# One routing table with 832 slots per expert in place of two tables with 640 and 240

## The chip, the cores and the metric

The kernel runs on one core of one Trainium2 chip. The metric is device time of one execution in microseconds (us), as the median of several runs. Inputs are float32 and float64 arrays (the first mixture's weights are float64 words that the kernel takes apart); the output is float32.

## The reference, cut to what matters

A linear attention with decays gives 3072 tokens of width 384. A first mixture takes the maximum of three products and projects back to 384. A second mixture routes each token to its two best of 8 experts and adds the weighted results:

```python
def _moe2_ref(x, w_gate, w_noise, noise, w1, w2):      # x: 3072 x 384, 8 experts, hidden width 1024
    logits = x @ w_gate
    noisy_logits = logits + np.log1p(np.exp(x @ w_noise)) * noise
    top2 = np.argpartition(-noisy_logits, 2, axis=1)[:, :2]
    # ... top2_w: softmax over the two
    for e in range(E):
        for k in range(2):
            mask = top2[:, k] == e
            h = np.maximum(x[mask] @ w1[e], 0.0)
            out[mask] += top2_w[mask, k, None] * (h @ w2[e])
```

## The kernel before

The program is one long straight line of tiles; a planner orders the instructions of each engine ahead of the run, by the order in the text and by its own durations for each instruction, and sets all semaphores.

First phase. Attention works in 24 half units; 12 units u of 256 tokens go through the first mixture (`ffn`, `proj`, lines 357 to 392). `proj` yields 128 tokens at a time, which an SP DMA writes to a gather table in DRAM (`x2d`), 392 words to a row: the token, then its weight for each expert. Batches b of six such tiles (768 tokens, four batches) are routed by `route_a` to `route_m` (lines 405 to 533), spread over the following units by `side`; the last batch is routed in the written order of the second phase. `route_c` counts, by matmuls, each token's rank among those of its expert; `route_r` adds the counts of the batches before (`base`); `route_h` makes two one-hot forms per tile and choice on DVE (rank within a block of 128, and block with expert, times the token's code); `route_m` multiplies them on TensorE and adds the result into a table `TAB` of [128 slots, block x expert]. `decode` turns the codes into row numbers `IDX` for the gathers and scatters.

Batches 0 to 2 are group 0 with a table of its own, a DRAM table of its own and 640 slots (5 blocks) per expert; batch 3 is group 1, with 240 slots (2 blocks).

Second phase (from line 724). The straight path gives each expert two parts, n = 2e and 2e + 1: part 0 has 384 tokens (blocks 0 to 2 of group 0), part 1 has 496 (blocks 3 and 4 of group 0, then 128 and 112 slots of group 1). For each tile of a part `gather` (line 755, POOL indirect DMA) fetches rows, `turn` (764) transposes them on TensorE and splits them into a high and a low part (ACT, DVE); for each of 8 slices of the hidden width `up` (781) runs 9 matmuls with all the part's tokens as moving columns (3 slices of the width, 3 products of high and low parts); for each tile `down` (800) runs 24 matmuls of 384 columns with the tile's hidden values as stationary operand, scales on ACT and adds the rows to the output by a POOL indirect DMA with accumulation. Each such scatter waits for the one before it. In steady state `up` of part n is interleaved with `down` of part n - 1 and `turn` of part n + 1, and part n + 2 is gathered.

The passage between the phases is written out by hand (lines 817 to 868): five gathers (three of part 0, two of part 1 of expert 0) stand ahead of the last `proj`; batch 3 is routed between the first `up` slices; then come the last two gathers of part 1 and those of part 2.

Slots without a token point at spare rows. An expert with more tokens than its slots is finished by `spill` (line 899) after all else, under a run-time branch on the counts `NBLK`.

Of the kernel before, what the change touches and what calls it, by code (L numbers as in the profile page):

```python
# [28 lines left out]
G_TILES = (18, 6)  # L29
G_HC = (18, 6)  # L30
G_SLOTS = (640, 240)
G_CAP = (5, 2)
G_MID = (1152, 0)   # a code's zero point within the group
G_FIRST = (0, 2304)
# float64's first word at 2 ** -127, as float32
# [4 lines left out]
def gla_moe_kernel(ctx: ExitStack, tc: tile.TileContext, qka, pad, vn, ws, wo, wgn, noise, e1, e2, out):  # L40
# [13 lines left out]
    # ---------------------------------------------------------------- constants  # L54
# [4 lines left out]
    iota = const.tile([128, 144], F32, name="iota")  # L59
    dumpc = const.tile([128, 2, 2], F32, name="dumpc")  # L60
# [4 lines left out]
    TAB = [const.tile([128, NE * G_HC[g]], F32, name=f"tab{g}") for g in range(2)]  # L65
    # rows of the group's gather table, rows of the output; empty slots take one of 128 more rows
    IDX = [const.tile([128, 2, NE * G_CAP[g]], I32, name=f"idx{g}") for g in range(2)]
    NBLK = [const.tile([128, NE], I32, name=f"nblk{g}") for g in range(2)]

    # ---------------------------------------------------------------- attention buffers  # L70
# [21 lines left out]
    # raw weights: two buffers, and three more in w_out's place until that is converted  # L92
# [34 lines left out]
    def late_consts():  # L127
        nc.gpsimd.memset(tri, 1.0)
        nc.gpsimd.affine_select(out=tri, in_=tri, pattern=[[1, 128]], compare_op=OP.is_gt, fill=0.0,
                                base=0, channel_multiplier=-1)  # L130
        nc.gpsimd.memset(ones, 1.0)
        nc.gpsimd.iota(iota, pattern=[[1, 144]], base=0, channel_multiplier=0,
                       allow_small_or_imprecise_dtypes=True)
        # a token's code: its place in its group, so numbered that zero is none's and
        # that float16 holds each
        nc.gpsimd.iota(code[:, 0:9], pattern=[[128, 9]], base=-1152, channel_multiplier=1,
                       allow_small_or_imprecise_dtypes=True)
        nc.gpsimd.iota(code[:, 9:18], pattern=[[128, 9]], base=1, channel_multiplier=1,
                       allow_small_or_imprecise_dtypes=True)
        nc.gpsimd.iota(code[:, 18:24], pattern=[[128, 6]], base=1, channel_multiplier=1,  # L140
                       allow_small_or_imprecise_dtypes=True)
        for g in range(2):
            for s, row in ((0, 128 * G_TILES[g]), (1, NT - G_FIRST[g])):
                nc.gpsimd.iota(dumpc[:, g, s:s + 1], pattern=[[1, 1]], base=row - G_MID[g],
                               channel_multiplier=1, allow_small_or_imprecise_dtypes=True)
            nc.gpsimd.memset(TAB[g], 0.0)

    def zero_rows(q):
# [4 lines left out]
        if q < 2:  # L153
            nc.sync.dma_start(x2d[q][128 * G_TILES[q]:], z)
# [3 lines left out]
    # float64 weights (as words) into a high and a low part of float32r each  # L158
    def dissect(raw, hi, lo):
# [3 lines left out]
        # magnitudes below float32's range become its zero; of those within, the exponent's  # L163
        # three bits after the first say nothing
# [31 lines left out]
    # w_out @ [w_gate | w_noise], as 16 further columns of w_out  # L196
# [51 lines left out]
        # product of a chunk's decays, for each e  # L248
# [71 lines left out]
        # the state before a chunk, decayed to its end  # L320
# [5 lines left out]
    def att_y(j):  # L326
# [13 lines left out]
        else:  # L340
# [6 lines left out]
            # the last pair's rows fill the gaps of the three others  # L347
# [5 lines left out]
    # ---------------------------------------------------------------- first mixture  # L353
# [21 lines left out]
    def proj(u, t):  # L375
# [14 lines left out]
        g = b // 3  # L390
        r = 128 * i - G_FIRST[g]
# [51 lines left out]
    def route_c(b):  # L443
        xf, oh, ob, ex = RT[b]
        g = b // 3
# [8 lines left out]
        # weights of the two  # L454
# [9 lines left out]
        r = 768 * b - G_FIRST[g]  # L464
        nc.sync.dma_start(x2d[g][r:r + 768, DM:XW].rearrange("(j p) e -> p j e", p=128), gs)
        RT[b] = [xf, oh, rk, ct]

    def route_r(b):
        """Rank of a token among those of its expert."""
        xf, oh, rk, ct = RT[b]  # L470
        rb = small([128, 6, NE], "rb")
        if b % 3 == 0:
            nc.vector.tensor_copy(rb, rk)
            nc.vector.tensor_reduce(base, ct.rearrange("p j e -> p e j"), axis=AX.X, op=OP.add)
        else:
# [3 lines left out]
            nc.vector.tensor_add(base, base, cs)  # L479
        rm = small([128, 6, 2, NE], "rm")  # L480
# [14 lines left out]
    def route_h(b, q):  # L495
        """One-hot forms of tiles 2q and 2q + 1: rank within a block, and block with expert."""
        lf, cf, held, ps = RT[b]
        n = NE * G_HC[b // 3]
        for j in (2 * q, 2 * q + 1):
            for k in range(2):  # L500
                A = small([128, 128], "A", F16, 8)
                C = small([128, 144], "C", F16, 8)
# [5 lines left out]
    def route_m(b, q):  # L508
        lf, cf, held, ps = RT[b]
        g = b // 3  # L510
        n = NE * G_HC[g]
# [12 lines left out]
        if g == 1:  # L524
            # left to the general path: none of the slots that the straight one takes
            nc.vector.memset(TAB[1][0:G_SLOTS[1] - 128, NE:2 * NE], 0.0)
        # blocks of the experts that need more than the straight path's slots
        nb = NBLK[g]
# [3 lines left out]
        nc.vector.tensor_scalar(full, base, float(G_SLOTS[g]), None, op0=OP.is_gt)  # L532
        nc.vector.tensor_mul(nb, nb, full)

    def decode(g, t, idx):
# [3 lines left out]
        nc.vector.tensor_scalar(p, t, 0.0, float(G_MID[g]), op0=OP.is_le, op1=OP.add)  # L539
# [319 lines left out]
    up(0, 5)  # L859
    up(0, 6)  # L860
    up(0, 7)
    down(0, 0)
    turn(1, 0)
    down(0, 1)
    turn(1, 1)
# [136 lines left out]
```

## Time and profile before

| what | value |
|---|---|
| runs: median, lowest, highest (3 runs) | 998.48, 997.84, 1000.98 us |
| profiled execution: span from the first to the last instruction | 996.3 us |
| profiled execution's own time beside the span | not listed apart from the span |
| PE (TensorE matmul) busy | 919.3 us (92%) |
| DVE, ACT, POOL busy | 516.7, 392.8, 331.1 us |
| mean granted TensorE clock | 0.985 |
| chain that ended last, by line | `up` L794 23%, `down` L808 22%, `ffn` L365 17% |

Engines: PE is TensorE's matmuls, PEld its weight loads (which overlap PE), DVE VectorE, ACT ScalarE, POOL GpSimd, SP SyncE. A matmul's listed duration holds its pipeline; what it costs in a stream is the distance from one start to the next, which the chain of waits shows for a run of them. A granted clock of 1.00 is TensorE's 2.4 GHz level, 0.50 its 1.2 GHz level. A name such as `psu<-xe,ew` gives the tile written and the tiles read, and L794 is a line of the kernel.

### The profile page before, as it was taken

The numbers are of one execution on the slowest core, as the hardware profiler recorded it, in microseconds if no ns is written. First come the engines' busy times: TensorE is split into PE (matmuls) and PEld (weight loads), VectorE is DVE, ScalarE is ACT, GpSimd is POOL, SyncE is SP. The second block draws the span as 40 slices with busy tenths as digits, with TensorE's granted clock in tenths as the row PEclk, the third lists the DMA queues.
The fourth block names the chain that finished last, engine by engine and source line by source line (L and its number), as shares of the span: only waits on it lengthen the run. The fifth ranks groups of instructions, "written<-read, shape, count | busy, mean of one in ns | idle before, by whom it ended". The sixth has DMA issues, their size and how long they took to land.

```text
span 996.3 us, 17883 instructions
## 1 busy us (share of the span) xinstructions
PE 919.3 (92%) x7186; PEld 870.9 (87%) x7187; DVE 516.7 (52%) x1043; ACT 392.8 (39%) x801; POOL 331.1 (33%) x366
## 2 busy tenths in 40 slices
PE   2367999999999999999899999999999999999994
PEld 2256899999999989999898999999999999999993
DVE  7999847786668865772574233332333332333110
ACT  4544544455445534632534233333333332333220
POOL 5565724322331332213116333323333332321212
PEclk9979999999999999999999999999999999999997
DMA  9642223135224332104434443433444434431122
GB/s 267 180 122 73 57 57 86 44 106 128 70 72 118 83 79 56 33 12 152 155 85 104 118 111 96 111 85 73 111 113 110 99 67 96 106 63 22 23 25 33
DMA packets 37352, 89.64 MB, mean 90 GB/s; under 512 B 8656, under 2 KB 25552, under 8 KB 37264
## 3 DMA queue, kind: packets, MB, share of 16 engines
q1 hardware_dynamic: 25744, 66.59, 23.7%
q0 software_dynamic: 11520, 21.86, 13.0%
q8 instruction: 58, 0.95, 0.4%
q14 instruction: 30, 0.25, 0.1%
HBM read 65.12 MB, written 20.95 MB: 86 GB/s over the span
## 4 chain that ended last, share of the span: by engine, by line
PE 75%; DVE 3%; DMA 3%; issue 1%; ACT 1%; SPq 0%; POOL 0%; POOLq 0%; ACTq 0%; DVEq 0%
PE psu L794 23%; PE psd L808 22%; PE p L365 17%; PE psl L380 5%; PE psx L775 2%; PE psS L292 1%; DMA out_dram<-y,idx 1%; PE psG L308 1%; PE psY L333 1%; DMA xt<-sg 1%; DMA raw<-in_e_dram 1%; PE psT L284 1%; PE psY L334 1%; DVE kh L241 0%; DVE st L318 0%
## 5 line engine op out<-in xcount | busy, mean ns | idle before, releaser
L365 PE MATMUL p<-xt,W 128*128 128x256 f32 x1944 | 254.0, 288 | 10.6 <-DVE m L369 3.9
L794 PE MATMUL psu<-xe,ew 128*128 128x496 f32 (+1 forms) x1152 | 251.8, 367 | 4.5 <-ACT xe L777 4.5
L365 PEld LDWEIGHTS p<-xt,W 128*128 128x128 f32 x1944 | 240.3, 193 | 16.3 <-DVE m L369 4.7
L808 PE MATMUL psd<-ew,he 128*128 128x384 f32 (+1 forms) x1344 | 244.1, 336 | 0.0
L808 PEld LDWEIGHTS psd<-ew,he 128*128 128x128 f32 (+1 forms) x1344 | 234.8, 186 | 1.7
L794 PEld LDWEIGHTS psu<-xe,ew 128*128 128x128 f32 x1152 | 206.7, 189 | 22.9 <-ACT xe L777 5.0
L798 DVE SCALAR_TENSOR_TENSOR he<-psu,he 128x496 fp32r<-128x496 f32 (+1 forms) x128 | 78.4, 614 | 267.9 <-ACT he L797 246.3
L813 POOL DMA_INDIRECT out_dram<-y,idx x56 | 88.4, 1578 | 181.9 <-ACT y L811 166.6
L373 POOL TENSOR_TENSOR H<-m,H 128x256 fp32r<-128x256 f32 x72 | 59.6, 828 | 189.8 <-ACT H L372 183.1
L797 ACT ACTIVATE he<-psu 128x496 fp32r<-128x496 f32 (+1 forms) x128 | 68.9, 539 | 115.7 <-PE psu L794 114.0
L811 ACT ACTIVATE y<-psd,GS 128x384 f32<-128x384 f32 (+1 forms) x56 | 32.5, 581 | 203.3 <-PE psd L808 199.7
L380 PE MATMUL psl<-WO,H 128*128 128x400 f32 x432 | 84.5, 348 | 0.0
L380 PEld LDWEIGHTS psl<-WO,H 128*128 128x128 f32 x432 | 76.8, 188 | 2.0 <-issue 1.3
L742 DVE TENSOR_TENSOR ew<-raw,ew 128x768 fp32r<-128x768 f32 x64 | 57.2, 954 | 33.1 <-ACT ew L741 32.8
L760 POOL DMA_INDIRECT xg<-x2d,idx x56 | 58.0, 1035 | 45.8 <-PE psx L775 21.3
L369 DVE TENSOR_TENSOR m<-p,m 128x256 f32<-128x256 f32 x72 | 30.0, 416 | 61.3 <-ACT m L368 58.1
L779 POOL COPY GS<-xg 128x1 f32<-128x1 f32 (+1 forms) x56 | 11.4, 271 | 135.1 <-DMA xg<-x2d,idx 135.0
L372 ACT CAST H<-m 128x256 fp32r<-128x256 f32 x72 | 29.2, 406 | 66.8 <-DVE m L370 66.8
L368 ACT COPY m<-p 128x256 f32<-128x256 f32 x72 | 26.5, 369 | 68.0 <-PE p L365 59.2
L741 ACT CAST ew<-raw 128x768 fp32r<-128x768 f32 x64 | 48.6, 834 | 3.0 <-DMA raw<-in_e_dram 3.0
L333 PE MATMUL psY<-x,la 128*64 128x64 f32 x384 | 31.0, 234 | 16.3 <-ACT la L323 14.6
L333 PEld LDWEIGHTS psY<-x,la 128*64 128x64 f32 x384 | 26.5, 145 | 20.4 <-ACT la L323 15.5
(152 smaller groups left out, 1081.9 us busy)
## 6 DMA issues: line engine op xcount, KB each, us to landing
raw<-in_e_dram SPq DMA_DIRECT2D x32, 768.0 KB, 6.7
qka<-in_qka_dram SPq DMA_DIRECT2D x48, 289.7 KB, 4.9
out_dram<-z SPq DMA_DIRECT2D x5, 960.0 KB, 5.3
vn<-in_vn_dram SPq DMA_DIRECT2D x24, 192.0 KB, 2.5
x2d<-x2t SPq DMA_DIRECT2D x24, 192.0 KB, 1.9
RAW<-in_ws_dram SPq DMA_DIRECT2D x5, 768.0 KB
wraw<-in_ws_dram SPq DMA_DIRECT2D x4, 768.0 KB, 5.5
xt<-sg SPq DMA_DIRECT2D x72, 32.0 KB, 2.3
```

The source lines that it names most:

```text
L333: nc.tensor.matmul(ps[0:64, p, s], LA[i][:, p, c], X1[j][:, sx], start=True, stop=True)
L365: nc.tensor.matmul(ps, W[:, f, w, a, k], x[:, k, b], start=n == 0, stop=n == 8)
L373: nc.gpsimd.tensor_sub(H[:, u % 2, f, 1], m, hi.bitcast(F32))
L380: nc.tensor.matmul(ps, H[:, u % 2, f, a, 128 * t:128 * t + 128], WOT[0][:, b, f], start=n == 0, stop=n == 17)
L741: nc.scalar.copy(hi, r)
L742: nc.vector.tensor_sub(EW[e, m][:, 1, s], r, hi.bitcast(F32))
L760: nc.gpsimd.indirect_dma_start(out=XG[n, i][0:w], out_offset=None, in_=x2d[g], in_offset=bass.IndirectOffsetOnAxis(ap=IDX[g][0:w, 0, c:c + ...
L794: nc.tensor.matmul(ps, w[:, a, f, k], XE[n][:, k, b], start=i == 0, stop=i == 8)
L797: nc.scalar.activation(hi, ps, AF.Relu)
L798: nc.vector.scalar_tensor_tensor(HE[n][:, f, 1], ps, 0.0, hi.bitcast(F32), op0=OP.max, op1=OP.subtract)
L808: nc.tensor.matmul(ps, HE[n][:, f, a, o:o + m], w[:, b, f], start=j == 0, stop=j == 23)
L813: nc.gpsimd.indirect_dma_start(out=out, out_offset=bass.IndirectOffsetOnAxis(ap=IDX[g][0:m, 1, c:c + 1], axis=0), in_=y, in_offset=None, c ...
```

## The change

The two groups become one: one table `TAB` of 24 blocks per expert, one DRAM table whose first 128 rows are the spare ones, codes around one zero point. The ranks of batch 3 go on where the others end, but not below 384 (`HEAD`), so that the first three blocks hold tokens of batches 0 to 2 only and can be decoded after batch 2. The straight path takes 832 slots per expert: 384 in part 0 and 448 in part 1 (tiles of 128, 128, 128 and 64). The table's width in `route_h` and `route_m` grows with the batch. All four gathers of a part 1 read the later index table; the first two of expert 0 move behind the routing of batch 3. The comments are gone. The core of the diff:

```diff
-G_SLOTS = (640, 240)
-G_CAP = (5, 2)
+NBK = 24
+HEAD = 384
+SLOTS = 832
+CAP = 7
...
-    x2d = [dram.tile([128 * G_TILES[g] + 128, XW], F32, name=f"x2d{g}") for g in range(2)]
+    x2d = dram.tile([128 + NT, XW], F32, name="x2d")
...
-        if q < 2:
-            nc.sync.dma_start(x2d[q][128 * G_TILES[q]:], z)
+        if q == 0:
+            nc.sync.dma_start(x2d[0:128], z)
...
-        nc.sync.dma_start(x2d[g][r:r + 128, 0:DM], x)
+        nc.sync.dma_start(x2d[128 * i + 128:128 * i + 256, 0:DM], x)
...
-        if b % 3 == 0:
+        if b == 0:
             nc.vector.tensor_copy(rb, rk)
...
+        if b == 2:
+            nc.vector.tensor_scalar(base, base, float(HEAD), None, op0=OP.max)
...
-        n = NE * G_HC[b // 3]
+        n = 6 * NE * (b + 1)
...
-        nc.vector.tensor_add(TAB[g], TAB[g], ps[:, 0:n])
-        if b < 2:
+        nc.vector.tensor_add(TAB[:, 0:n], TAB[:, 0:n], ps[:, 0:n])
+        h = NE * HEAD // 128
+        if b == 2:
+            decode(TAB[:, 0:h], IDX[0])
+        if b < 3:
             return
-        n = NE * G_CAP[g]
-        decode(g, TAB[g][:, 0:n], IDX[g])
+        decode(TAB[:, h:NE * CAP], IDX[1])
...
-    PARTS = (((0, 0, 128, 0), (0, 1, 128, 128), (0, 2, 128, 256)),
-             ((0, 3, 128, 0), (0, 4, 128, 128), (1, 0, 128, 256), (1, 1, G_SLOTS[1] - 128, 384)))
-    SIZE = (384, 256 + G_SLOTS[1])
+    PARTS = (((0, 128, 0), (1, 128, 128), (2, 128, 256)),
+             ((3, 128, 0), (4, 128, 128), (5, 128, 256), (6, SLOTS % 128, 384)))
+    SIZE = (HEAD, SLOTS - HEAD)
...
-            out=XG[n, i][0:w], out_offset=None, in_=x2d[g],
-            in_offset=bass.IndirectOffsetOnAxis(ap=IDX[g][0:w, 0, c:c + 1], axis=0))
+            out=XG[n, i][0:w], out_offset=None, in_=x2d if h else x2d[0:128 + LATE],
+            in_offset=bass.IndirectOffsetOnAxis(ap=IDX[h][0:w, 0, c:c + 1], axis=0))
...
     gather(0, 2)
-    gather(1, 0)
-    gather(1, 1)
     proj(10, 0)
...
     route_m(3, 2)
+    gather(1, 0)
+    gather(1, 1)
     gather(1, 2)
     gather(1, 3)
...
     down(0, 0)
+    down(0, 1)
     turn(1, 0)
-    down(0, 1)
     turn(1, 1)
+    down(0, 2)
     turn(1, 2)
     turn(1, 3)
-    down(0, 2)
```

## Rows read from the trace of the kernel before

**Rows 1.** Stretches: length, busy us (instructions) PE, PEld, DVE, ACT, POOL; clock, DMA, GB/s.
```profile
0.00:60.00 60.00, 17.52 (x221) 14.82 (x222) 51.42 (x69) 27.00 (x47) 34.64 (x48) 0.93 0.71 196
...
420.00:480.00 60.00, 60.00 (x583) 58.09 (x583) 29.65 (x93) 18.75 (x44) 15.84 (x24) 1.00 0.23 71
...
620.40:680.70 60.30, 60.30 (x336) 57.37 (x335) 19.83 (x31) 20.68 (x38) 19.80 (x21) 1.00 0.44 98
```

**Rows 2.** Chain of waits within one expert: start us, length us, what.
```profile
628.78 0.29 PE psx L775 x3
629.07 1.57 PE psu L794 x9
630.65 4.18 PE psd L808 x24
...
636.87 0.33 PE psx L775 x3
637.20 2.02 PE psu L794 x9
639.22 4.17 PE psd L808 x24
```

**Rows 3.** Groups by line and form, PE: table matmuls (busy us, mean ns | idle before).
```profile
L516 PE MATMUL pstab<-r_C,r_A 128*128 128x144 f16 x36 | 3.8, 229 | 0.0
...
L516 PE MATMUL pstab<-r_C,r_A 128*128 128x48 f16 x12 | 2.2, 194 | 0.0
```

**Rows 4.** The page's groups: weight loads of `up`.
```profile
L794 PEld LDWEIGHTS psu<-xe,ew 128*128 128x128 f32 x1152 | 206.7, 189 | 22.9 <-ACT xe L777 5.0
```

**Rows 5.** Timeline of the passage, all engines: start us, length us, instruction [idle before <-releaser].
```profile
454.80 0.95 POOL L760 DMA_INDIRECT xg<-x2d,idx  x1 [0.30 <-issue]
...
514.68 0.31 DVE L504 TENSOR_SCALAR r_C<-iota,r_cf,code 128x48 f16<-128x48 f32 x1
...
518.96 0.20 PE L516 MATMUL pstab<-r_C,r_A 128*128 128x48 f16 x1
...
520.31 1.00 POOL L760 DMA_INDIRECT xg<-x2d,idx  x1 [0.76 <-DVE r_z L542]
...
520.75 4.42 PE L808 MATMUL psd<-ew,he 128*128 128x384 f32 x24
...
524.13 0.95 POOL L760 DMA_INDIRECT xg<-x2d,idx  x1 [0.30 <-issue]
...
525.73 0.81 ACT L777 CAST xe<-psx 128x384 fp32r<-128x384 f32 x2
...
526.60 1.17 PE L794 MATMUL psu<-xe,ew 128*128 128x496 f32 x4 [0.81 <-ACT xe L777]
```

**Rows 6.** Timeline of POOL: a gather of 112 rows, and the copy that waits for it.
```profile
569.92 0.97 POOL L760 DMA_INDIRECT xg<-x2d,idx  x1 [0.31 <-issue]
573.53 0.18 POOL L779 COPY GS<-xg 112x1 f32<-112x1 f32 x1 [2.64 <-DMA xg<-x2d,idx]
```

**Rows 7.** Groups by line and form, DVE: the forms of block with expert.
```profile
L504 DVE TENSOR_SCALAR r_C<-iota,r_cf,code 128x144 f16<-128x144 f32 x36 | 12.8, 360 | 0.0
...
L504 DVE TENSOR_SCALAR r_C<-iota,r_cf,code 128x48 f16<-128x48 f32 x12 | 3.5, 304 | 0.0
```

**Rows 8.** Stretches around PE's wait for the first expert's weights.
```profile
492.50:494.50 2.00, 0.04 (x1) 0.00 (x0) 0.27 (x1) 0.34 (x1) 0.00 (x0) 1.00 1.04 403
494.50:496.20 1.70, 0.00 (x0) 0.00 (x0) 1.18 (x2) 1.70 (x5) 0.00 (x0) 0.90 1.03 404
496.20:498.00 1.80, 1.77 (x6) 1.77 (x7) 1.73 (x5) 1.78 (x3) 0.00 (x0) 0.50 0.87 358
498.00:500.00 2.00, 2.00 (x10) 2.00 (x10) 1.35 (x5) 1.71 (x4) 0.00 (x0) 0.68 0.90 262
```

**Rows 9.** Timeline of the end: the last two scatters.
```profile
980.81 1.54 POOL L813 DMA_INDIRECT out_dram<-y,idx  x1 [3.47 <-DMA out_dram<-y,idx]
...
986.16 1.47 POOL L813 DMA_INDIRECT out_dram<-y,idx  x1 [3.81 <-DMA out_dram<-y,idx]
```

More of the change, by code (lines that the diff above doesn't have):

```diff
@@ L64, in gla_moe_kernel @@
     wg = const.tile([128, 3, 16], F32, name="wg")
-    TAB = [const.tile([128, NE * G_HC[g]], F32, name=f"tab{g}") for g in range(2)]
-    IDX = [const.tile([128, 2, NE * G_CAP[g]], I32, name=f"idx{g}") for g in range(2)]
-    NBLK = [const.tile([128, NE], I32, name=f"nblk{g}") for g in range(2)]
+    TAB = const.tile([128, NE * NBK], F32, name="tab")
+    IDX = [const.tile([128, 2, NE * n], I32, name=f"idx{g}") for g, n in enumerate((HEAD // 128, CAP - HEAD // 128))]
+    NBLK = const.tile([128, NE], I32, name="nblk")
     QKA = [at.tile([128, 1545], F32, name=f"qka{i}") for i in range(2)]
@@ L131, in late_consts @@
         nc.gpsimd.memset(ones, 1.0)
-        nc.gpsimd.iota(iota, pattern=[[1, 144]], base=0, channel_multiplier=0,
+        nc.gpsimd.iota(iota, pattern=[[1, 192]], base=0, channel_multiplier=0,
                        allow_small_or_imprecise_dtypes=True)
-        nc.gpsimd.iota(code[:, 0:9], pattern=[[128, 9]], base=-1152, channel_multiplier=1,
+        nc.gpsimd.iota(code[:, 0:12], pattern=[[128, 12]], base=-MID, channel_multiplier=1,
                        allow_small_or_imprecise_dtypes=True)
-        nc.gpsimd.iota(code[:, 9:18], pattern=[[128, 9]], base=1, channel_multiplier=1,
+        nc.gpsimd.iota(code[:, 12:24], pattern=[[128, 12]], base=1, channel_multiplier=1,
                        allow_small_or_imprecise_dtypes=True)
[L140 to L146, printed above, removed]
+        for k, row in enumerate((-128, NT)):
+            nc.gpsimd.iota(dumpc[:, k:k + 1], pattern=[[1, 1]], base=row - MID,
+                           channel_multiplier=1, allow_small_or_imprecise_dtypes=True)
+        nc.gpsimd.memset(TAB, 0.0)
     def zero_rows(q):
@@ L501, in route_h @@
                 A = small([128, 128], "A", F16, 8)
-                C = small([128, 144], "C", F16, 8)
+                C = small([128, 192], "C", F16, 8)
                 nc.vector.tensor_scalar(A, iota[:, 0:128], lf[:, j, k:k + 1], None, op0=OP.is_equal)
@@ L531, in route_m, with decode @@
         nc.vector.tensor_scalar(nb, nb, 7, None, op0=OP.logical_shift_right)
-        nc.vector.tensor_scalar(full, base, float(G_SLOTS[g]), None, op0=OP.is_gt)
+        nc.vector.tensor_scalar(full, base, float(SLOTS), None, op0=OP.is_gt)
         nc.vector.tensor_mul(nb, nb, full)
-    def decode(g, t, idx):
+    def decode(t, idx):
         n = t.shape[1]
@@ L538, in decode @@
         z = small([128, 40], "z")[:, 0:n]
-        nc.vector.tensor_scalar(p, t, 0.0, float(G_MID[g]), op0=OP.is_le, op1=OP.add)
+        nc.vector.tensor_scalar(p, t, 0.0, float(MID), op0=OP.is_le, op1=OP.add)
         nc.vector.scalar_tensor_tensor(p, p, -1.0, t, op0=OP.add, op1=OP.add)
-        for i in range(2):
-            nc.vector.tensor_scalar(z, t, 0.0, dumpc[:, g, i:i + 1], op0=OP.is_equal, op1=OP.mult)
-            nc.vector.scalar_tensor_tensor(idx[:, i], p, float(i * G_FIRST[g]), z, op0=OP.add, op1=OP.add)
+        for i, first in enumerate((128, 0)):
+            nc.vector.tensor_scalar(z, t, 0.0, dumpc[:, i:i + 1], op0=OP.is_equal, op1=OP.mult)
+            nc.vector.scalar_tensor_tensor(idx[:, i], p, float(first), z, op0=OP.add, op1=OP.add)
     prep_a(0)
@@ L811, in down @@
         nc.scalar.activation(y, ps, AF.Copy, scale=GS[0:m, n, i:i + 1])
-        c = blk * NE + e
+        c = (blk - PARTS[h][0][0]) * NE + e
         nc.gpsimd.indirect_dma_start(
-            out=out, out_offset=bass.IndirectOffsetOnAxis(ap=IDX[g][0:m, 1, c:c + 1], axis=0),
+            out=out, out_offset=bass.IndirectOffsetOnAxis(ap=IDX[h][0:m, 1, c:c + 1], axis=0),
             in_=y, in_offset=None, compute_op=OP.add)
@@ L896, in gla_moe_kernel, with spill @@
             turn(*j)
-    def spill(g, blk, e):
+    def spill(blk, e):
         w1 = p2.tile([128, 3072], F32, tag="ew", name="w1s", bufs=3)
@@ L933, in spill @@
             in_=y, in_offset=None, compute_op=OP.add)
-    both = small([128, NE], "both", I32)
-    nc.vector.tensor_add(both, NBLK[0], NBLK[1])
     more = small([128, 1], "more", I32)
-    nc.vector.tensor_reduce(more, both, axis=AX.X, op=OP.max)
-    with tc.If(nc.values_load(more[0:1, 0:1], min_val=0, max_val=sum(G_HC)) > 0):
-        for g in range(2):
-            with tc.For_i(0, NE, 1) as e:
-                n = nc.values_load(NBLK[g][0:1, bass.ds(e, 1)], min_val=0, max_val=G_HC[g])
-                with tc.For_i(G_SLOTS[g] // 128, n, 1) as blk:
-                    spill(g, blk, e)
+    nc.vector.tensor_reduce(more, NBLK, axis=AX.X, op=OP.max)
+    with tc.If(nc.values_load(more[0:1, 0:1], min_val=0, max_val=NBK) > 0):
+        with tc.For_i(0, NE, 1) as e:
+            n = nc.values_load(NBLK[0:1, bass.ds(e, 1)], min_val=0, max_val=NBK)
+            with tc.For_i(SLOTS // 128, n, 1) as blk:
+                spill(blk, e)
 def layout(q, k, v, alpha, moe_w1, moe_w2, moe_w3, moe_w_out, moe2_w_gate, moe2_w_noise, moe2_noise,
```

39 lines of the change are left out of this document (16 added, 23 removed).

## The prediction

> **What bounds the kernel now.** I read first the busy time by stage. From 180 us on TensorE (PE) is busy in nearly the whole of every stretch, in the last 60 us of the first mixture and in an expert's 60 us of the second mixture alike, at granted clock 1.00 (its 2.4 GHz level), while DVE, ACT and POOL are at a quarter to a half and the DMA engines at 0.23 to 0.44 [rows 1]. The chain of waits, followed in order of time, says the same: inside an expert it consists of PE pieces alone, laid end to end. There 9 up matmuls over 384 columns take 1.57 us, 9 over 496 columns 2.02 us, 24 down matmuls 4.17 to 4.18 us, and the three transposes of a turn 0.33 us [rows 2]. So in the second mixture time is the sum of PE's slots, and what doesn't shorten them gains nothing. Three stretches go by other limits: the start, where PE works 17.5 of 60 us [rows 1]; the passage into the second mixture, where PE needs gathered tokens [rows 5]; and the end, where the scatters go one after the other [rows 9].
>
> **The wide part shrinks (496 to 448 columns).** In each expert's second part `up` runs 8 x 9 matmuls over SIZE[1] columns; 8 experts make 576. A slot is 2.02/9 = 224.4 ns at 496 columns and 1.57/9 = 174.4 ns at 384 [rows 2]. At the granted clock the columns alone would take 206.7 and 160.0 ns, so the surplus is 17.7 and 14.4 ns. On the line between the two rows 448 columns take 174.4 + 64/112 x 50.0 = 203.0 ns; with either surplus it is 186.7 + 14.4 = 201.1 or 186.7 + 17.7 = 204.4 ns. Saved: 576 x 21.4 ns = **12.4 us** (11.5 to 13.4). I take the line, since 448 lies between both rows. All of it is on the path, as PE has no gap there to hide it in. ACT and DVE copies get shorter too, and gain nothing.
>
> The Trainium skill (TensorE: Matmul & The Clock Gate, section Back-to-back issue gap) gives the spacing in a stream of weight loads and matmuls as 81 ns at 128 columns and 131 ns at 512. By that slope, 0.13 ns per column, 48 columns would be worth an estimated 576 x 6.3 ns = 3.6 us. The trace does not bear it out here: its slope between 384 and 496 is 0.45 ns per column, and its slot at 496 is 224 ns [rows 2].
>
> **Downs and turns.** The number of down tiles stays at 7 per expert, and each still streams 384 columns; only the last tile has 64 stationary columns, not 112. Such a tile of 112 takes 4.18 us where one of 128 takes 4.17 [rows 2], so I cost this at 0 (a gain is bounded by nothing nearer than that equality; I allow 0.2 us). The last turn's transposes go from 112 to 64 tokens: 128 to 112 gives 0.33 to 0.29 us [rows 2], 48 tokens more at that slope 0.12 us, 8 times 1.0 us; a floor under a small transpose would leave 0. I take **0.8 us**, nearer to the slope.
>
> **The table matmuls and their one-hot forms.** The width n was 144 for batches 0 to 2 and 48 for batch 3; it becomes 48, 96, 144, 192. A table matmul lasts 229 ns at 144 and 194 at 48 [rows 3], 0.36 ns per column. Batch 0 saves 12 x 35 ns, batch 1 half of that: together **0.6 us** of PE in the first mixture, where it is full, of which I count 0.5. The DVE forms there shrink as well (360 against 304 ns [rows 7]) and gain nothing beside PE. Batch 3 gets 144 columns more: +52 ns in each of 12 matmuls, +0.6 us, and 12 forms longer by 144 x 0.58 = 84 ns, +1.0 us of DVE. Both belong to the passage below.
>
> **Setup and tail.** One zero-row DMA and four small POOL setup instructions go; at the start PE waits for longer work than these, and I put 0 (0 to 0.5). The `max` on `base` and the shorter decode of batch 2 are single small DVE instructions beside full PE. At the end the scatters of one expert part start over 5 us apart (the last two 5.35), each waiting for the one before [rows 9]; that stays, and the fourth is now of 64 rows. A scatter of 112 rows occupies POOL for 1.47 us against 1.54 for 128 [rows 9], so 48 rows fewer save 0.2 us there, and something in landing: **0.4 us** (0 to 1.0).
>
> **The passage: what is given back.** Before, two of the four gathers for expert 0's second part were issued around 455 us [rows 5], 65 us ahead of need, because they read the first table. Now all four read `IDX[1]`, which exists only after batch 3's last table matmul. On POOL nothing else waits behind them but the next gathers, a scatter and the gate copies, none of which PE needs earlier; the two places freed at 455 us let the first mixture's H halves through sooner, and PE doesn't wait for those.
> What PE needs is the fourth tile, since each `up` matmul takes all 448 columns. Before: last table matmul at 518.96, first gather at 520.31, then one every 1.27 us (three steps to 524.13); PE had a down tile from 520.75 to cover the landing and started `up` at 526.60, after 0.81 us idle that ended with ACT's copies, not with a DMA [rows 5].
> After: the first gather moves by +0.6 (wider table matmuls), -0.3 (one turn that stood before them goes behind), and +0.1 us (table addition over 144 columns more and decode over 16 more, at the forms' 0.58 ns per column [rows 7]). The wider DVE forms cost nothing on hardware: the last one starts at 514.68, 4 us ahead of the last matmul [rows 5]. But the order is a planner's, which may set the matmuls later by up to that 1.0 us; I take 0.5. So +0.9: the fourth gather starts at 525.0. It lands 3.6 us after its start (569.92 to 573.53 [rows 6]), at 528.6; a turn and its copy take about 1.0 us (0.33 on PE, 0.4 on ACT, hand-overs). `up` starts at 529.6 where it started at 526.60: **+3.0 us**. The cover, one down tile of 4.2 us, is the same size as before; the wait behind it grows from 0.8 to about 3.8 us. Bounds: 0 if the planner finds other work for PE, and 8.8 if two more things come on top (rivals below).
>
> **Sum.** -12.4 - 0.8 - 0.5 - 0.4 + 3.0 = -11.1 us. The span is 996.3 us; nothing else is listed for that execution, and the median of the runs, 998.48, lies 2.2 above it. I set the sum against the median: **987.4 us**.
>
> **Rivals.**
> 1. *The new idle time costs clock as well.* When PE stood idle from 492.5 to 496.2, the granted clock was 0.50 in the next 1.8 us and 0.68 in the 2 us after [rows 8]: 0.9 + 0.6 us of lost work, some 1.6 us. The wait now expected is as long, but transposes fall into it. Then 989.0. If the planner also puts the turns ahead of the down tile, so that 4.2 us of cover come too late, 993.2.
> 2. *The passage is free*: the planner moves other ready work there. Against: until the fourth tile there is only one down tile. 984.4.
> 3. *Slots don't shrink with the columns* but hang on the weight loads (189 ns each [rows 4]). Against: 174 ns slots at 384 columns are shorter than a load. If nothing were saved by `up`, 999.8; if half, 993.6. The skill's slope named above would make it an estimated 996.2.
> 4. *The spare path runs (slower).* The straight path now holds 832 tokens per expert, both batches' groups together. From the 833rd token of any expert on, `spill` runs after all else: two weight loads of 1.57 MB, at the 404 GB/s that the loads reached [rows 8] 7.8 us, a gather of 3.6 and a scatter of 5.3 us [rows 6, 9], and between them turn, ups and a down in series, some 5 us: over 21 us, so 1009. For it: the slack fell. Against: counting the reference's choices for these inputs gives 744 to 812 tokens per expert, and with 550 to 608 in the first three batches none is lifted by the floor of 384.
> 5. *The planner's order changes elsewhere.* It orders by its own durations, several of which change; a changed wait in the first mixture could give or take 2 to 4 us around the forecast.
>
> **Chances.** Forecast 0.55 (its own range 986 to 990), rival 1 0.20, rival 2 0.07, rival 3 0.04, rival 4 0.03, rival 5 0.11. Eight times in ten the time should lie between 984.0 and 993.0: from the free passage to the passage with both additions, and the bounds of `up` (11.5 to 13.4) inside. Less than 0.3%, 3 us, can't be told from no change. Faster by more: all but rival 4, most of rival 3 and a bad tail of rival 5: 0.92. Within: 0.03. Slower: 0.05.
>
> **What would show it.** Groups of 9 up matmuls over 448 columns at 1.81 to 1.84 us; an expert's period down from 60.2 to about 58.5 us; from the last table matmul to the first `up` of expert 0's second part about 10 us, not 7.6, with PE idle for over 3 us and the clock row telling rival 1; the last scatters still 5 us apart. Wrong would be: up slots above 210 ns, any instruction of `spill`, or the first mixture ending later than before by over 2 us.

## The result: 990.13 us, 8.9 us less than before

| kernel | median of its runs | lowest, highest | profiled execution | its span |
|---|---|---|---|---|
| before (4 runs) | 998.99 us | 997.84, 1000.98 | 998.48 us | 996.3 us |
| changed (4 runs) | 990.13 us | 987.89, 992.08 | 989.96 us | 988.3 us |

Ratio 0.9908, 95% interval 0.9886 to 0.9930. The forecast was 987.4 with a range of 984.0 to 993.0: the direction and the range held, and the measured time lies 2.7 us above the forecast. The rest is about where the missing gain went, since its terms are much larger than their sum. Two stray runs, one of 1159.54 us of the kernel before and one of 3504.03 us in experiment 7, stand in none of the medians and intervals here.

Four milestones of the two profiled executions cut the span into parts that can be compared: the first `up` of expert 0's first part, the first `up` of its second part, and ACT's first `y` of the last part.

| stretch | before | after | difference | forecast |
|---|---|---|---|---|
| start to first `up` of part 0 | 496.23 | 494.21 | -2.0 | -0.5 |
| from there to first `up` of part 1 (the passage) | 30.37 | 33.84 | +3.5 | +3.0 |
| from there to `y` of the last part | 443.31 | 434.92 | -8.4 | -13.2 |
| from there to the end | 26.39 | 25.33 | -1.1 | -0.4 |
| span | 996.3 | 988.3 | -8.0 | -11.1 |

So the loss against the forecast sits in the long third stretch (4.8 us), and the first gives 1.5 of it back. The busy time by stage of the changed kernel (columns as in [rows 1]) shows PE filled as before; one expert is now 59.05 us long, where it was 60.2 to 60.3:

```profile
420.00:480.00 60.00, 60.00 (x582) 58.09 (x581) 28.89 (x85) 17.29 (x41) 13.62 (x20) 1.00 0.21 62
602.00:661.05 59.05, 59.05 (x335) 56.35 (x334) 19.28 (x31) 20.20 (x38) 19.92 (x22) 1.00 0.40 98
```

The chain of waits inside one expert of the changed kernel (start, length, what) answers to [rows 2]. The wide `up` groups fell from 2.02 to 1.82 to 1.85 us, which is 202 to 206 ns a slot: the term that carries the forecast is there in full. The surprise is the group behind the last turn. Turn and group together took 0.29 + 1.57 = 1.86 us before with 112 tokens; here, with 64, they take 0.33 + 1.77 = 2.10 us:

```profile
627.57 1.56 PE psu L792 x9
629.13 0.33 PE psx L773 x3
629.46 1.77 PE psu L792 x9
631.22 4.17 PE psd L806 x24
635.39 1.83 PE psu L792 x9
637.22 0.33 PE psx L773 x3
637.55 1.83 PE psu L792 x9
639.38 4.18 PE psd L806 x24
643.56 1.85 PE psu L792 x9
```

The timeline of the weight loads (PEld) shows what is special there. Before, the loads of a 112-token turn began at 628.45, ahead of the turn's place on PE at 628.78 [rows 2]. After, PEld stands idle for 0.25 us "for issue", that is for nothing that the profile shows, and starts only at 629.06:

```profile
628.45 0.41 PEld L775 LDWEIGHTS psx<-ident,xg 112*128 112x128 f32 x3
```

```profile
629.06 0.26 PEld L773 LDWEIGHTS psx<-ident,xg 64*128 64x128 f32 x3 [0.25 <-issue]
```

**The passage after**, as a timeline of all engines (columns as in [rows 5]). Look at POOL first: a scatter of expert 0's part 0 stands at 518.71, so that the first of the four late gathers starts at 520.66, though its index is written at 519.40 + 0.19. Then PE: a down tile until 522.95, and from there four turns, each waiting for its own gather, and `up` at 528.05.

```profile
518.01 0.51 PE L512 MATMUL pstab<-r_C,r_A 128*128 128x192 f16 x4
518.49 4.46 PE L806 MATMUL psd<-ew,he 128*128 128x384 f32 x24
518.55 0.36 DVE L515 TENSOR_TENSOR tab<-tab,pstab 128x192 f32<-128x192 f32 x1 [1.92 <-PE pstab L512]
518.71 1.65 POOL L811 DMA_INDIRECT out_dram<-y,idx  x1 [37.37 <-ACT y L809]
519.40 0.19 DVE L540 SCALAR_TENSOR_TENSOR idx<-r_p,r_z 128x32 int32<-128x32 f32 x1
520.66 1.00 POOL L758 DMA_INDIRECT xg<-x2d,idx  x1 [0.31 <-issue]
...
524.26 0.52 PE L773 MATMUL psx<-ident,xg 128*128 128x128 f32 x3 [1.31 <-DMA xg<-x2d,idx]
524.48 0.92 POOL L758 DMA_INDIRECT xg<-x2d,idx  x1 [0.30 <-issue]
525.38 0.52 PE L773 MATMUL psx<-ident,xg 128*128 128x128 f32 x3 [0.60 <-DMA xg<-x2d,idx]
526.59 0.52 PE L773 MATMUL psx<-ident,xg 128*128 128x128 f32 x3 [0.69 <-DMA xg<-x2d,idx]
527.27 0.37 PE L773 MATMUL psx<-ident,xg 64*128 64x64 f32 x3 [0.17 <-DMA xg<-x2d,idx]
528.05 1.16 PE L792 MATMUL psu<-xe,ew 128*128 128x448 f32 x3 [0.41 <-ACT xe L775]
```

The stretches of the passage, first before, then after: PE's idle time in it grew from 30.37 - 29.56 = 0.81 to 33.84 - 30.66 = 3.18 us, and its busy time by 1.1.

```profile
496.23:526.60 30.37, 29.56 (x176) 27.92 (x176) 19.82 (x96) 12.05 (x23) 6.45 (x6) 0.95 0.39 111
```

```profile
494.21:528.05 33.84, 30.66 (x175) 28.04 (x176) 21.45 (x96) 12.25 (x23) 7.36 (x7) 0.95 0.33 95
```

**The clock behind it.** The third number from the end is the granted clock. Before, it stayed at 1.00 from 526 to 534. After, it falls to 0.62 and 0.53 in the four microseconds from 528: 0.76 + 0.94 = 1.7 us of PE's work lost. This is what rival 1 describes.

```profile
526.00:528.00 2.00, 1.40 (x8) 1.21 (x9) 0.97 (x2) 0.54 (x2) 1.39 (x3) 1.00 0.58 169
528.00:530.00 2.00, 2.00 (x11) 1.68 (x11) 0.51 (x1) 0.48 (x1) 1.70 (x2) 1.00 0.61 151
530.00:532.00 2.00, 2.00 (x11) 1.67 (x10) 0.05 (x1) 0.00 (x0) 1.85 (x8) 1.00 0.56 87
```

```profile
526.00:528.00 2.00, 0.89 (x6) 0.57 (x6) 0.90 (x2) 1.21 (x3) 1.59 (x2) 1.00 0.48 126
528.00:530.00 2.00, 1.95 (x8) 1.70 (x8) 0.48 (x2) 0.00 (x0) 1.49 (x2) 0.62 0.56 148
530.00:532.00 2.00, 2.00 (x8) 1.79 (x7) 0.56 (x1) 0.48 (x1) 1.85 (x8) 0.53 0.54 92
532.00:534.00 2.00, 2.00 (x12) 1.85 (x11) 0.62 (x1) 0.54 (x1) 1.83 (x3) 1.00 0.74 123
```

**The end** answers to [rows 9]: the scatters still start about 5 us apart, each waiting for the landing of the one before, and the last, of 64 rows, occupies POOL for 1.42 us.

```profile
973.76 1.54 POOL L811 DMA_INDIRECT out_dram<-y,idx  x1 [3.38 <-DMA out_dram<-y,idx]
978.86 1.42 POOL L811 DMA_INDIRECT out_dram<-y,idx  x1 [3.56 <-DMA out_dram<-y,idx]
```

### The profile page after: what moved, and what is told of

The parts are those of the page before. It is cut to its first block, busy times and chain, and to the rows that moved or that the text cites. A ratio compares the mean times of both kernels' runs of the same rounds, so it can differ in the third digit from the quotient of the medians.

```text
span 988.3 us, 17871 instructions
## 1 busy us (share of the span) xinstructions
PE 913.0 (92%) x7186; PEld 866.7 (88%) x7187; DVE 514.6 (52%) x1040; ACT 389.5 (39%) x801; POOL 329.3 (33%) x362
## 4 chain that ended last, share of the span: by engine, by line
PE 74%; issue 4%; DMA 3%; DVE 2%; POOL 0%; ACT 0%; POOLq 0%; ACTq 0%; DVEq 0%
PE psd L806 21%; PE psu L792 21%; PE p L363 18%; PE psl L378 5%; DMA out_dram<-y,idx 2%; PE psx L773 2%; PE psS L290 1%; PE psG L306 1%; PE psY L331 1%; PE psT L282 1%; DMA xt<-sg 1%; PE psY L332 1%; DVE kh L239 0%; DVE x L259 0%; DMA xg<-x2d,idx 0%
## 5 line engine op out<-in xcount | busy, mean ns | idle before, releaser
L792 PE MATMUL psu<-xe,ew 128*128 128x448 f32 (+1 forms) x1152 | 242.5, 358 | 4.3 <-ACT xe L775 4.3
L806 PEld LDWEIGHTS psd<-ew,he 128*128 128x128 f32 (+1 forms) x1344 | 227.0, 180 | 8.1 <-ACT y L809 0.2
L796 DVE SCALAR_TENSOR_TENSOR he<-psu,he 128x448 fp32r<-128x448 f32 (+1 forms) x128 | 75.5, 590 | 265.0 <-ACT he L795 265.0
L795 ACT ACTIVATE he<-psu 128x448 fp32r<-128x448 f32 (+1 forms) x128 | 66.3, 518 | 112.3 <-PE psu L792 112.3
```

Of the source, the lines that this page charges most:

```text
L792: nc.tensor.matmul(ps, w[:, a, f, k], XE[n][:, k, b], start=i == 0, stop=i == 8)
L795: nc.scalar.activation(hi, ps, AF.Relu)
L796: nc.vector.scalar_tensor_tensor(HE[n][:, f, 1], ps, 0.0, hi.bitcast(F32), op0=OP.max, op1=OP.subtract)
L806: nc.tensor.matmul(ps, HE[n][:, f, a, o:o + m], w[:, b, f], start=j == 0, stop=j == 23)
```

## The experiments

The theory was: the fewer columns of `up` give the whole gain and more, and the merge of the tables by itself costs time, through the passage. The rival was that the merge pays too, by fewer table matmuls and less setup. The first two runs separate the sizes from the merge; the next take the changed kernel's losses one by one. A period is the distance between the same group of two successive experts.

**1. The sizes alone: `e1_narrow_two_tables`.** The kernel before, its two tables kept, with 624 and 208 slots; part 1 has tiles of 128, 112, 128 and 80. The 112 table entries that a shorter tile leaves over are cleared.

```diff
-G_SLOTS = (640, 240)
+G_SLOTS = (624, 208)
...
+        if g == 0:
+            nc.vector.memset(TAB[0][0:112, 4 * NE:5 * NE], 0.0)
...
-             ((0, 3, 128, 0), (0, 4, 128, 128), (1, 0, 128, 256), (1, 1, G_SLOTS[1] - 128, 384)))
-    SIZE = (384, 256 + G_SLOTS[1])
+             ((0, 3, 128, 0), (0, 4, 112, 128), (1, 0, 128, 240), (1, 1, 80, 368)))
+    SIZE = (384, 448)
```

> Two tables kept, 624 + 208 slots, so that the second part has 448 columns without the merge (tiles of 128, 112, 128, 80). Theory (narrower up saves some 12 us; the merge costs the passage some 5 us, of which 1.7 by the fallen clock; a last turn on few rows costs 0.2 us more instead of 0.1 less): 986 to 988.5 us, up(1,0) about 30.4 us after the first up as before, no clock fall there. Rival (the merge costs nothing, the up slots simply save less than 12 us): same as the changed kernel, 990 us.

Measured: 986.76 us (before 999.85 on the same chip), ratio 0.9877 (0.9857 to 0.9898). From the first `up` of part 1 to the last part's `y` it takes 430.96 us, 12.35 less than before, with the clock at 1.00 behind the passage in both. The expectation missed one thing: the passage is not as before but 32.13 us, 1.76 longer, though the late gathers start only 0.45 us later behind the first `up`. PE waits for ACT's copies, and ACT's last copy starts late for a reason that the profile calls only "remote" (ACT, then PE):

```profile
527.62 0.36 ACT L779 CAST xe<-psx 128x240 fp32r<-128x240 f32 x1 [0.95 <-remote]
528.03 1.07 PE L796 MATMUL psu<-xe,ew 128*128 128x448 f32 x4 [2.23 <-ACT xe L779]
```

The chain of waits shows what an 80-token turn costs: 0.21 + 1.60 = 1.81 us.

```profile
744.49 0.21 PE psx L777 x3
744.70 1.60 PE psu L796 x9
746.30 4.23 PE psd L810 x24
750.53 1.83 PE psu L796 x9
```

These sizes alone bring 13.1 us, more than the whole change, and the lowest median of all kernels here. They aren't quite the sizes of the changed kernel: the last turn has 80 tokens, not 64, which by the chains shown is worth 2.10 - 1.81 = 0.29 us in each of seven turns, less 0.06 that a down tile of 80 takes longer (4.23 against 4.17): some 1.6 us. Of the 4 us between the two kernels' third stretches (434.92 and 430.96), that and the 1.7 us of clock are most.

**2. The merge alone: `e2_merge_wide`.** The changed kernel with `SLOTS = 880`, so 496 columns and a last tile of 112, as before.

```diff
-SLOTS = 832
+SLOTS = 880
```

> The merge alone: one table with 880 slots, second part 496 columns and a last tile of 112 as before. Theory: slower than the kernel before by the passage, 3.5 us idle and 1.7 us clock, less what the first mixture may give back (0 to 2): 1001 to 1004 us. Rival (the merge costs nothing): 997 to 999 us.

Measured: 1001.98 us, ratio 1.0023 (1.0014 to 1.0032): the merge by itself costs some 2 us (1.4 to 3.2), and here too the clock fell behind the passage (0.50 and 0.70). By the four stretches of the table above, its profiled execution differs from before by -2.1, +3.9, +1.6 and -0.6 us. The two ratios' distances from 1 add up to -1.23 + 0.23 = -1.0%; the change has -0.92%. So the theory stands, and the rival, that the merge pays, falls.

**3 and 4. The 64-token turn: `e3_turn_128` and `e6_turn80`.** In the changed kernel the last tile of a part 1 is gathered and transposed with 128, or 80, rows; what `up` reads is the same 448 columns. (For 80 rows, `r = max(w, 80)` stands for 128.)

```diff
-            out=XG[n, i][0:w], out_offset=None, in_=x2d if h else x2d[0:128 + LATE],
-            in_offset=bass.IndirectOffsetOnAxis(ap=IDX[h][0:w, 0, c:c + 1], axis=0))
+            out=XG[n, i], out_offset=None, in_=x2d if h else x2d[0:128 + LATE],
+            in_offset=bass.IndirectOffsetOnAxis(ap=IDX[h][:, 0, c:c + 1], axis=0))
...
-            nc.tensor.transpose(ps[:, 128 * k:128 * k + w], x[0:w, 128 * k:128 * k + 128], ident[0:w, 0:w])
+            nc.tensor.transpose(ps[:, 128 * k:128 * k + 128], x[:, 128 * k:128 * k + 128], ident)
```

> The changed kernel, but the last tile of a part gathers 128 rows and is transposed at 128 rows; 64 of them are used. Theory (the weight load for a 64-row transpose isn't loaded ahead and costs about 0.3 us per expert): 2 to 2.6 us faster than the changed kernel, near 988 us, expert period 58.7 us where it was 59.05. Rival (what the expert period lost lies elsewhere): 990 us, period unchanged.

> The changed kernel, but a part's last tile gathers and transposes 80 rows (64 used), not 64. Theory (a 64-row transpose costs 0.3 us per expert more than one of 80 rows, and a gather of 80 rows lands hardly later than one of 64, where 128 rows did): period 58.75 us for 59.05, time 987.8 to 988.5 us. Rival (what the turn gives, the passage takes again, as with 128 rows): 990 us.

Measured: 128 rows 990.43 us (0.9906; 0.9893 to 0.9919), period 58.83; 80 rows 989.23 us (0.9897; 0.9880 to 0.9915), period 58.72, where the changed kernel has 59.05. The chain of waits of the kernel with 128 rows shows the doubled turn cheaper than the 64-token one, 0.33 + 1.59 = 1.92 us against 2.10:

```profile
747.63 0.33 PE psx L773 x3
747.95 1.59 PE psu L792 x9
```

So a larger turn is faster, as expected, and the period shows it in both. The total doesn't follow: the passage is 34.96 and 34.66 us, about 1 longer, and the clock is low for longer (with 128 rows 0.50 from 526 to 532). Of 1.5 to 2.3 us in the experts, nothing or 0.9 us arrives in the median. That the larger turn lengthens the passage isn't shown, though: a second profile of the changed kernel itself (experiment 11) has a passage of 35.14 us.

**5. One gather less in the passage: `e4_head_512`.** The floor under batch 3's ranks is 512, so that four blocks are known early; the first gather of part 1 is issued before the last `proj`, and its turn comes ahead of the second down tile.

```diff
+EARLY = 512
...
-            nc.vector.tensor_scalar(base, base, float(HEAD), None, op0=OP.max)
+            nc.vector.tensor_scalar(base, base, float(EARLY), None, op0=OP.max)
...
     gather(0, 2)
+    gather(1, 0)
     proj(10, 0)
...
     down(0, 0)
-    down(0, 1)
     turn(1, 0)
+    down(0, 1)
     turn(1, 1)
```

> The changed kernel with the floor of ranks at 512, so that four blocks are decoded after batch 2 and the first gather and turn of expert 0's second part go back to their early place. Theory (the passage waits for the fourth gather, 1.27 us apart): up(1,0) 1.2 us earlier, and 1.7 us more if the clock then doesn't fall: 987 to 989 us. Rival (the passage is set by something else, the routing or ACT): 990 us, the same wait.

Measured: 990.28 us (0.9893; 0.9878 to 0.9908), a miss. The passage is 33.62 us, only 0.2 shorter. The last table addition comes 24.95 us behind the first `up` (at 519.74), where it was 24.34, so that the last of now three late gathers starts at 524.23, 29.44 us behind the first `up` against 30.27: of the 1.25 us that a gather's place on POOL takes, 0.8 is left. PE still waits 1.36 us for its first late turn, and the clock falls all the same, here while the last turns run (0.60 from 526 to 528).

**6. More cover: `e5_dummy`.** The changed kernel with 12 extra matmuls of 384 columns, whose result nothing reads, written behind the third down tile.

```diff
     down(0, 2)
+    psz = pm.tile([128, 512], F32, tag="p3", name="psz")[:, 0:384]
+    for j in range(12):
+        nc.tensor.matmul(psz, HE[0][:, 7, 0, 0:128], EW[0, 1].rearrange("p a (f d) -> p a f d", f=8)[:, 0, 7],
+                         start=j == 0, stop=j == 11)
```

> The changed kernel with 12 more matmuls of 384 columns (2.1 us, result unused) behind the last down tile of expert 0's first part, where PE waits for the gathers. Theory (of the passage's cost 1.6 us is the clock that fell after PE's waits): the clock stays at 1.00 and the time falls to 988.5 us in spite of more work. Rival (only the wait counts): no gain, 990 to 991 us.

Measured: 996.9 us (0.9973; 0.9963 to 0.9983); both expectations missed by far, and this was the most instructive run. The planner put the extra matmuls between the last table matmuls (518.88 to 521.6), so that they delayed the table instead of covering the gathers, and it set a second scatter ahead of the gathers on POOL. That scatter waits for the first to land, and the gathers, in order behind it, wait too:

```profile
519.59 1.65 POOL L811 DMA_INDIRECT out_dram<-y,idx  x1 [37.87 <-ACT y L809]
524.77 1.56 POOL L811 DMA_INDIRECT out_dram<-y,idx  x1 [3.53 <-DMA out_dram<-y,idx]
526.63 1.01 POOL L758 DMA_INDIRECT xg<-x2d,idx  x1 [0.30 <-issue]
```

From the table addition (521.13) to the first gather it is 5.50 us, where the changed kernel has 2.11; the addition itself comes 27.05 us behind the first `up`, 2.7 later than there. The first turn then waits 4.48 us for its gather, the passage is 40.45 us, and the clock falls here too. It doesn't tell whether cover would keep the clock up; it shows that what stands ahead of the gathers on POOL can lengthen the passage by several us.

**7 and 8. Real work as cover: `e7_fill`, `e8_fill80`.** Expert 1's part 0 is gathered and turned early, its weights split early, and two of its `up` slices are written ahead of expert 0's part 1; the second kernel has the 80-row turn as well.

```diff
     gather(0, 2)
+    gather(2, 0)
+    gather(2, 1)
+    gather(2, 2)
     proj(10, 0)
...
     down(0, 1)
+    turn(2, 0)
+    turn(2, 1)
+    turn(2, 2)
+    down(0, 2)
+    up(2, 0)
     turn(1, 0)
     turn(1, 1)
-    down(0, 2)
+    up(2, 1)
     turn(1, 2)
```

> The changed kernel with real work in the passage: expert 1's first part is gathered early (its index table exists after batch 2), its turns, its weights' split and two of its up slices stand before expert 0's second part. Theory (the passage costs 3.2 us of PE waits and 1.7 us of clock): both go, 985 us. Rival (the planner or the weights put the work elsewhere, or the wait moves behind it): 988 to 990 us.

> The two before together: work in the passage and last tiles of 80 rows. Theory (both costs are separate): 982.5 to 983.5 us, faster than the changed kernel by 7 us and than the kernel before by 16. Rival: not better than the better of the two alone.

Measured: 991.67 us (0.9932; 0.9912 to 0.9951) and 990.49 us (0.9907; 0.9893 to 0.9921); both theories miss. The fill runs, but the wait only moves behind it, as the first rival had it. In PE's timeline with 80 rows the last turn of part 1 is at 530.34, and `up` starts 4.64 us behind its end. ACT copies that part's last two tiles only at 532.89 and 535.04, after waits that the profile again calls "remote"; what it waits for isn't known (PE, then ACT):

```profile
530.34 0.42 PE L774 MATMUL psx<-ident,xg 80*128 80x80 f32 x3 [0.86 <-DVE xe L777]
535.41 1.86 PE L793 MATMUL psu<-xe,ew 128*128 128x448 f32 x4 [4.64 <-issue]
```

```profile
532.89 0.48 ACT L776 CAST xe<-psx 128x384 fp32r<-128x384 f32 x1 [0.96 <-remote]
535.04 0.32 ACT L776 CAST xe<-psx 128x192 fp32r<-128x192 f32 x1 [1.67 <-remote]
```

**9 and 10. POOL's order: `e9_pool_order`, `e10_pool_turn80`.** The scatters of expert 0's part 0 read a copy of their index that is made behind batch 3's decode, so none can stand ahead of the late gathers; four `y` tiles in place of two keep the downs from waiting. The second kernel has the 80-row turn as well.

```diff
+    IDXS = const.tile([128, 24], I32, name="idxs")
...
+        nc.vector.scalar_tensor_tensor(IDXS, IDX[1][:, 1, 0:24], 0.0, IDX[0][:, 1], op0=OP.mult, op1=OP.add)
...
-        y = pr.tile([128, DM], F32, tag="y", name="y", bufs=2)[0:m]
+        y = pr.tile([128, DM], F32, tag="y", name="y", bufs=4)[0:m]
...
-            out=out, out_offset=bass.IndirectOffsetOnAxis(ap=IDX[h][0:m, 1, c:c + 1], axis=0),
+            out=out, out_offset=bass.IndirectOffsetOnAxis(
+                ap=IDXS[0:m, c:c + 1] if n == 0 else IDX[h][0:m, 1, c:c + 1], axis=0),
```

> Changed kernel, but the scatters of expert 0's part 0 read their rows from a copy of the index that is made behind batch 3's decode, so that none of them can stand ahead of the late gathers on POOL; four y tiles, not two, so that the downs don't wait for them. In the changed kernel the first late gather starts at 520.66 though its index is there at 519.6, because a scatter of 1.65 us stands before it. Theory (the order on POOL's queue sets the passage): the first late gather starts about 0.1 us behind the index, up(1,0) comes about 1 us earlier, 988.5 to 989.3; if the shorter waits also keep the granted clock at 1.00, 987 to 987.7. Rival (the passage hangs on the landing and the turn alone, or the planner uses the freed place for something else): up(1,0) within 0.3 us of the changed kernel's 33.8 us behind the first up, 990.

> The same, and each expert's last tile gathered and turned with 80 rows instead of 64. Theory: the expert's period is 58.7 us as with 80 rows alone (59.05 in the changed kernel), 2 us over seven turns, and the passage is as short as with the new order alone, so 986 to 987.5. Rival: as with 80 rows alone, where the passage gave 0.8 us back, 989.

Measured: 990.45 us (0.9920; 0.9906 to 0.9934) and 990.25 us (0.9914; 0.9894 to 0.9934). In the median neither gains anything. Locally the theory holds. The timeline of the first (DVE, then POOL) has the first late gather 1.31 us behind the last table addition; in the changed kernel it is 520.66 - 518.55 = 2.11:

```profile
519.34 0.35 DVE L516 TENSOR_TENSOR tab<-tab,pstab 128x192 f32<-128x192 f32 x1 [1.92 <-PE pstab L513]
```

```profile
520.65 0.99 POOL L760 DMA_INDIRECT xg<-x2d,idx  x1 [39.02 <-DVE r_z L541]
```

From the table addition to `up` it is 9.00 us, and 8.71 with 80 rows, against 9.50 in the changed kernel. But in the first the table addition itself came 24.84 us behind the first `up`, against 24.34, which takes the gain back, so that the whole passage was 33.84 us again and the rival's number came out; with 80 rows the passage is 33.18 us. The second kernel's median hides a spread from 986.8 to 994.0 us; its profiled execution, at 987.9, is near its lower end, with a period of 58.85 where 58.7 was expected.

**11 and 12. The same two kernels once more: `e11_after_again`, `e12_order_again`.** In the first profiles of the changed kernel and of experiment 9 the passage was equally long, 33.84 us, but the clock fell in one and stayed up in the other. A second profiled execution of each asks whether that belongs to the kernel.

> The changed kernel itself, a second profiled execution, beside the kernel with the scatters of part 0 behind the late gathers: in the first profiles both had a passage of 33.84 us, but the granted clock fell to 0.62 and 0.53 behind it in the one and stayed at 1.00 in the other. Theory (the fall belongs to the order of the work in the passage): the clock falls again in the four microseconds behind up(1,0), and up(1,0) to the last part's y again takes 434.9 us. Rival (it differs from execution to execution): the clock may stay at 1.00, and then that stretch takes 433.3 to 433.7 us.

> The kernel with the scatters of part 0 behind the late gathers and four y tiles, unchanged, a second profiled execution. Theory (the order of the work decides over the clock): granted clock 1.00 throughout 520 to 536 us again, and 433.6 us from up(1,0) to the last part's y. Rival (execution to execution): the clock falls this time, and the stretch takes about 435 us.

Measured: the changed kernel's clock fell again (0.80, 0.50, 0.50, 0.50 from 526 to 534; passage 35.14 us, from there to the last `y` 435.49, 991.96 us in all). So the same kernel's passage differs by 1.3 us between two executions. Experiment 9's kernel kept it in its first profile and lost it in its second, here in this order:

```profile
528.00:530.00 2.00, 1.66 (x9) 1.52 (x10) 0.82 (x2) 0.50 (x3) 1.48 (x2) 1.00 0.58 151
530.00:532.00 2.00, 2.00 (x11) 1.86 (x10) 0.57 (x2) 0.81 (x2) 1.87 (x7) 1.00 0.54 96
```

```profile
528.00:530.00 2.00, 2.00 (x9) 1.78 (x8) 0.04 (x1) 0.40 (x1) 1.70 (x2) 0.62 0.62 145
530.00:532.00 2.00, 2.00 (x7) 1.77 (x7) 0.56 (x1) 0.08 (x1) 1.84 (x8) 0.53 0.59 86
```

From `up` to the last `y` these two took 433.65 and 435.28 us: 1.6 us for the clock, as rival 1 had priced it. Their passages were 33.84 and 33.08 us. For the kernel of experiment 9 the fall differs from execution to execution. The second profile also repeats that kernel's local gain (first gather 1.31 us behind the table addition, 8.75 us from there to `up`, against 9.83 in the changed kernel of the same chip).

## Why the prediction was right, and where its size was off

**`up` at 448 columns: right.** Forecast -12.4 us (11.5 to 13.4; 576 x 21.4 ns is 12.3). In the chain each of an expert's eight wide groups fell from 2.02 to 1.82 to 1.85 us: 64 x 0.18 to 0.19 = some 12.0 us. Experiment 1 shows the same without the merge: -12.35 us in that stretch, in which the 80-row turn's 0.05 us per expert goes back into its down tile (4.23 us, before 4.18). The measured slope is (2.02 - 1.83) / 9 / 48 = 0.44 ns per column, on the line between the two rows, and rival 3 fell. The page of the Trainium skill that the forecast weighed (TensorE: Matmul & The Clock Gate, section Back-to-back issue gap), whose slope would have given an estimated 3.6 us, does not describe this stream. The down tiles cost nothing more, as forecast: one of 64 tokens takes 4.17 us.

**The turns: wrong, and the largest single error.** The forecast had: "The last turn's transposes go from 112 to 64 tokens: 128 to 112 gives 0.33 to 0.29 us [rows 2], 48 tokens more at that slope 0.12 us, 8 times 1.0 us". The cost isn't a slope. Turn and next group take 1.92 us at 128 rows, 1.86 at 112, 1.81 at 80 and 2.10 at 64. So 64 rows cost 0.24 us more than 112 in each of the seven turns in steady state, +1.7 us in place of -0.8. The allowed bound ("a floor under a small transpose would leave 0") excluded a loss, with no reason that a row gave. Experiments 3 and 4 showed the period falling from 59.05 to 58.83 and 58.72 when the turn is made larger. In the profile the surplus goes with a weight load that no longer starts ahead; why the chip does that at 64 rows and not at 80 was not settled.

**The clock: rival 1 came true**, for which the forecast had given a chance of 0.20 and 1.6 us; 1.7 us were lost in the profiled execution. The measured 990.13 us lies just outside the forecast's own 986 to 990, and near rival 1's 989.0. The third stretch now adds up: -12.0 + 1.7 + 1.7 = -8.6, measured -8.4.

**The passage: right in size, with errors that mostly cancel.** +3.5 us measured, +3.0 forecast; the idle time grew from 0.8 to 3.2 us where 3.8 was written. From the last table matmul to `up` about 10 us were forecast and some 9.8 came. But the fourth gather starts 30.27 us behind the first `up`, where 28.8 had been worked out from 525.0. Some 0.6 of these 1.5 us come from the table addition: it starts at 518.55, 1.4 us later behind the first `up` than before (519.20), where the forecast's terms ahead of it make 0.8. The forecast's remark that "on POOL nothing else waits behind them but the next gathers, a scatter and the gate copies" looked at what stands behind the gathers and not at what the planner may set ahead: the scatter at 518.71 is one, and it is worth 0.8 us (experiment 9). That scatter is no newcomer: before, one started at 517.89, ended ahead of the index and delayed nothing. In return the 64 rows of the last tile landed 2.66 us after the gather's start, where 3.6 had been taken from a gather of 112 rows [rows 6].

**First mixture and tail: better than forecast.** -2.0 in place of -0.5: in all profiles of kernels with one table the first `up` came at 494.1 to 494.8, with two tables at 495.9 to 496.2. The table matmuls at 48 and 96 columns have nearly their forecast means (186 and 208 ns against 229 at 144). What else changed isn't in one place: PE's idle time differs by -4.6 us from 0 to 60, +2.4 from 60 to 120 (where the mean clock is 0.86, before 0.95), and by -0.4, +0.8, -0.8 and -0.4 in the four stretches of 60 us behind that. No run takes these apart. The tail gave -1.1 in place of -0.4, some 0.3 in the landings of the first three scatters and the rest behind the last.

**Sum of the errors**: turns +2.5, clock +1.7, passage +0.5, `up` +0.4, first mixture -1.5, tail -0.7: +2.9, against 11.1 - 8.0 = 3.1 in the spans. Part of this is luck: 5.1 us of costs that the sum didn't hold were met by 2.2 us of gains that it didn't hold either, so the total came nearer to the forecast than its terms did.

Rivals 2 (free passage) and 4 (spare path) didn't come: PE waited 3.2 us in the passage, and no weight load or gather follows the last scatter.

**What stays open.** Whether the clock falls behind the passage isn't decided by its length alone: in the two profiles of before and of experiment 1 it stayed, in the twelve with one table it fell eleven times, and the twelfth is the first of experiment 9. PE's waits ahead of `up` add up to 0.81 us in before, 2.23 in experiment 1 (one piece) and 2.72 in that profile of experiment 9. Where the clock fell they add up to 2.36 (experiment 10), 2.44 (experiment 12) and up to 6.31 us (experiment 8). The changed kernel's 3.2 us are spread between short turns. A wait of 3.21 us in one piece (experiment 7) was followed by a fall too, so the spread isn't needed for one. Another reading is that the turns between the waits hold the clock no better than waiting does: from the last down matmul to `up` PE has only turns and waits for 5.10 us in the changed kernel, 4.32 and 4.37 in experiments 10 and 12, 4.61 in the profile that kept the clock, 2.76 in experiment 1. No run here isolates either; the experiments that were to fill the gap moved it instead. Open as well are ACT's "remote" waits, 0.95 us in experiment 1 and 0.96 and 1.67 in experiment 8, each ahead of a late `up`.

## What to carry to other kernels

Take a change apart by its own parts before judging it: here smaller tiles gave 13.1 us (with a last turn of 80 tokens), and the merge that made them natural cost 2. The kernel with smaller tiles and the old tables has the lowest median, 986.76 us, though its interval (0.9857 to 0.9898) still touches that of the change (0.9886 to 0.9930). When work is moved behind a late result, ask what the planner can set ahead of it on the same in-order queue, not only what comes behind; one scatter in front of the gathers cost 0.8 us here, two cost 4.2 (5.50 us from the table addition to the first gather, against 1.31 with none). A smaller instruction isn't a cheaper one until a row of that size shows it. And a stretch that differs by 1.3 us between two executions of one kernel needs more than one profile before a change of 1 us in it is explained.

## What the hardware showed that was not expected

- Three transposes of 64 rows, with the nine matmuls behind them, took 2.10 us, more than those of 80 (1.81), 112 (1.86) or 128 rows (1.92); PEld waited 0.25 us before the loads of the 64-row ones.
- The granted clock fell from 1.00 to 0.5 to 0.6 for three to four microseconds behind some 3 us of waits spread over 5 us, and did not behind one wait of 2.23 us; in one kernel it did so in one of two profiled executions, behind 2.44 us of waits and not behind 2.72.
- An accumulating scatter behind another waits for its landing: 519.59 to 524.77 in experiment 6, with the late gathers, whose index was written by 522.2, behind it on POOL.
